# Output and next state in one step, two copies dropped, whole-tile units in the second tile, and the last output in three parts

## The chip, the cores and the metric

The kernel runs on one core of one Trainium2 chip. The time is device microseconds, the median of three runs of the whole program. In the profile PE is the matrix engine and PEld its weight loads, DVE, ACT and POOL are the three elementwise engines, and SP issues the DMAs.

## The reference

Three stages run one after the other on 4 sequences of 768 positions. The first is a chunked linear attention with decay (8 heads of 32 columns, state of 16 rows a head); its output, seen as 3072 tokens of 256 values, goes through two feed-forward layers.

```python
cum = np.cumsum(la, axis=-1)                          # per chunk, la = log(clip(a))
L = np.exp(cum[:, :, :, None] - cum[:, :, None, :]) * causal
M = np.einsum('bhin,bhjn->bhij', Cc, Bc) * L
y = np.einsum('bhij,bhjd->bhid', M, xc) + np.einsum('bhin,bhnd->bhid', Cc, state) * exp(cum)
state = decay_full * state + sum_j(Bc x xc * decay_from_j)
...
h = np.maximum(np.maximum(x @ w1, x @ w2), x @ w3)    # d_ff 768, float64 weights
x = h @ w_out
h = x @ w_in                                          # d_ff 2048
g = np.maximum(h, 0.0) + alpha * np.minimum(h, 0.0)
out = g @ w_out
```

## The kernel before

The tokens are cut into six tiles of 512. The attention is cut into 24 **rounds** of 128 positions of one sequence, so four rounds make a tile's input `xt`. A round has these pieces of PE work, with the lines by which the profile shows them: transposes T of the inputs (L331), the products CB of the two state vectors (L422 in rounds 0 to 11, L412 from round 12 on, where the round is one chunk of 128 instead of two of 64), the output Y (L496 and L504, later L480 and L483), and the state update U (L455, later L441). Around them ACT takes the exponentials (L400, L395), DVE multiplies (L427, L414) and writes `xt` (L514), POOL masks and scales, and SP loads the inputs `b`, `c`, `xm` and the decay rows `e`. From round 12 on, SP also sends two operands through DRAM and back into `bs` and `cs`, and `att_r` then copies both on DVE onto themselves (L372).

The feed-forward work is cut into **units**, one block of 128 hidden features for a number of tokens. Every fp32 product is made of three products of rounded halves, so a first-layer unit has 18 products `up` (3 weights, 2 halves of the input, 3 terms) and 6 products `down` (`acc`), all on L572; a second-layer unit has 6 and 6. `PHASES` gives the order: first layer of tiles 0 and 1, then second layer of tile 0, first layer of tile 2, and so on. Tiles 0 and 1 are cut into two units of 256 tokens for each feature block (`SPLIT`, 12 units a tile), the others into units of 512.

The weights come as float64. They are fetched in 28 pieces of 512 KB into the three `st` buffers, and `convert` turns each piece into two float32 halves in four steps on DVE and ACT (L156 to L171). `next_weights(pace)` hands out one step after each product group.

The order is written in Python: after each unit `quota` says how many attention steps of the list `todo` are due so that the rounds are done when a tile needs them, and `until` forces those that are late. A step is one lambda of `rounds`. A scheduler then moves instructions ahead where its own model of the engines says that they are ready, so each engine's order isn't word for word that of the Python loop; on the chip each engine takes its instructions in that fixed order.

Of the kernel before, what the change touches and what calls it, by code (L numbers as in the profile page):

```python
# [9 lines left out]
F32 = mybir.dt.float32  # L10
# [4 lines left out]
AF = mybir.ActivationFunctionType  # L15
# [4 lines left out]
P = 128  # L20
BT, H, S, D, N = 4, 8, 768, 32, 16
DM = H * D
# [3 lines left out]
NR = BT * NB  # L26
FF1, FF2 = 768, 2048
NF1, NF2 = FF1 // P, FF2 // P
NT = BT * S // 512

SPLIT, WHOLE = ((0, 256), (256, 256)), ((0, 512),)
PHASES = [(1, 0, SPLIT, 1), (1, 1, SPLIT, 1)]
for _t in range(NT):
    PHASES += [(2, _t, WHOLE, 1)] + [(1, _t + 2, WHOLE, 1)] * (_t + 2 < NT)

LEAD = 6144
START = 4
LAG = 2
NX = 3

C_ID, C_PAR, C_PM, C_N = 0, 128, 130, 132
C_TU, C_TS, C_TW, C_SEL, C_T = 0, 128, 256, 512, 1024
NPA = 2
SUMS = 0
WIDE = 20
ORDER = [(0, 0), (1, 0), (0, 1), (1, 1), (2, 0), (2, 1)]
BW = 2
WARM = 8
# [23 lines left out]
def fused(ctx: ExitStack, tc: tile.TileContext, x, a, B, C, w1, w2, w3, w_out, v_in, v_out, alpha, cst, out):  # L72
    nc = tc.nc
# [41 lines left out]
    def st_tile():  # L115
        return stage.tile([P, 1024], U32, tag="st", name="st", bufs=3)
# [60 lines left out]
    steps = convert()  # L177
    ready = [0]

    def need(i):  # L180
        while ready[0] <= i:
            next(steps)

    def next_weights(n):
        for _ in range(n):
            next(steps, None)


    cum_d = dr.tile([NQ, BT * H, Q], F32, name="cum_d", bufs=1)
# [86 lines left out]

    def wide_sums(half):

        if half == 0:
            nc.sync.dma_start(s_c[:, C_TW:C_SEL], cst[:, C_N + C_TW:C_N + C_SEL])  # L280
        ks = slice(3 * half, 3 * half + 3)
        cols = slice(3 * P * half, 3 * P * (half + 1))
        pc = ptile(ps_at, "at", (BT * H, 3 * P))
        for k in range(3):
            nc.tensor.matmul(pc[:, k * P:(k + 1) * P], s_la[:, 3 * half + k, :], s_c[:, C_TW:C_TW + P], start=True, stop=True)
        nc.scalar.activation(s_a[:, cols], pc, AF.Copy)
        nc.sync.dma_start(cum_w[:, cols], s_a[:, cols])
# [64 lines left out]
    def att_l(r):  # L352
# [6 lines left out]
        for c in range(4):  # L359
# [4 lines left out]
                cs[o].bitcast(F32).rearrange("q v e t -> q v (e t)"),  # L364
                sc[:, h:h + 2, :].rearrange("(v q) e t -> q v (e t)", v=4),
            )

    def att_r(r):
        if r < NDIR:
            return  # L370
        for t in (blk[r]["bs"], blk[r]["cs"]):
            nc.vector.tensor_copy(t, t.bitcast(F32))  # L372

    def first_e(r):

# [141 lines left out]
    def rounds(r0):  # L517

        for r in range(r0, NR):
            def first(r=r):  # L520
                if r + 1 < NR:
                    att_l(r + 1)
                if r + 2 < NR:
                    att_a(r + 2)
            yield first, 0
            yield lambda r=r: att_y(r), r + 1
            if r + 1 < NR:
                yield lambda r=r: att_e(r + 1), 0
                yield lambda r=r: (att_r(r + 1), att_u(r + 1)), 0
                yield lambda r=r: att_b(r + 1), 0  # L530
            if r + 2 < NR:
                yield lambda r=r: (att_t(r + 2), load(r + 3)), 0
# [8 lines left out]
    def until(blocks):  # L541
        while y_done[0] < blocks:
            attend()
# [5 lines left out]
    def units_of(ph):  # L549

        layer, t, tokens = ph[:3]
        if len(tokens) == 1:
            cut = [(f, 0, 512) for f in range(NF1 if layer == 1 else NF2)]
        else:
            cut = [(f, *tokens[h]) for q, h in ORDER for f in (2 * q, 2 * q + 1)]
        return [(f, o, n, (24 if layer == 1 else 12) * n, (4 * t + (o + n) // P) * (layer == 1)) for f, o, n in cut]

    def quota(i):

        most, ahead, own = 0.0, 0, plan[i][3]  # L560
        for _, _, _, cols, blocks in plan[i:]:
            most = max(most, left(blocks) * own / max(own, ahead - LEAD))
            ahead += cols
        return most


    def parts(acc, wh, wl, rhs, first, last):
# [16 lines left out]
        return gh[:, :n], gl[:, :n]  # L584

    def up1(ph, f, o, n):
        t, pace = ph[1], ph[3]
        fs = slice(f * P, (f + 1) * P)
        g = un.tile([P, 512], F32, tag="g", name="g")[:, :n]
        for j in range(3):  # L590
            need(4 * (f // 2) + j)
            p = up_mm([w[:, j, :, fs] for w in w123], xt[t], o, n)
            if j == 0:
                nc.scalar.activation(g, p, AF.Copy)  # L594
            else:
                nc.vector.tensor_tensor(g, p, g, ALU.max)  # L596
            next_weights(pace)
        return halves(g, n)

    def up2(ph, f, o, n):  # L600
        t, pace = ph[1], ph[3]
# [6 lines left out]
        next_weights(pace)  # L608
        return halves(g, n, nc.vector if t == NT - 1 and f == NF2 - 1 else nc.gpsimd)

    acc = {}
# [24 lines left out]
    def end2(ph, lo=0, n=512):  # L636
        t = ph[1]
        z = [v_tile().bitcast(F32) for _ in range(2)]
        nc.scalar.activation(z[0][:, :n], acc[2, t][0][:, lo:lo + n], AF.Copy)
        nc.vector.tensor_copy(z[1][:, :n], acc[2, t][1][:, lo:lo + n])  # L640
        base = 512 * t + lo

        def finish(i):
            p = ps_up.tile([P, 2, DM], F32, tag="up", name="up")
            for j in range(2):
# [3 lines left out]
            o = st_tile().bitcast(F32)[:, :512].rearrange("p (j d) -> p j d", j=2)  # L649
            if i % 2:  # L650
                nc.vector.tensor_copy(o, p)
            else:
                nc.scalar.activation(o, p, AF.Copy)
            row = base + 2 * i * P
            nc.sync.dma_start(out[row:row + 2 * P, :].rearrange("(j p) d -> p j d", p=P), o)
        tail.extend(lambda i=i: finish(i) for i in range(n // 256))

    junk = ps_up.tile([P, 512], F32, tag="up", name="up")

# [60 lines left out]
    if True:  # L720
        nc.sync.dma_start(alph, alpha.rearrange("(k p) -> p k", p=P))
        todo += [(go, 0) for go in (
            lambda: att_a(2), lambda: (att_t(2), load(3)), lambda: att_e(2),
            lambda: att_u(2), lambda: att_b(2), lambda: att_a(3), lambda: (att_t(3), load(4)),
        )]
        todo.insert(SUMS, (lambda: list(sums(1)), 0))
        todo += rounds(2)
        for i, go in enumerate((lambda: wide_sums(0), lambda: wide_sums(1), wide_back)):
            todo.insert(WIDE + 3 * i, (go, 0))
        plan = [u for ph in PHASES for u in units_of(ph)]  # L730

        owed, at = 0.0, 0
        for ph in PHASES:
            layer, t, _, pace = ph
            up, end = (up1, end1) if layer == 1 else (up2, end2)
            pend = []
            for f, o, n, _, blocks in units_of(ph):
                until(blocks)
                pend.append((f, o, n, up(ph, f, o, n)))
# [6 lines left out]
                next_weights(pace)  # L746
                owed += quota(at)
                at += 1
                while owed > 0.999 and todo:
                    owed -= 1  # L750
                    attend()
            for i, u in enumerate(pend):
                def go(ph=ph, u=u, finish=end if i == LAG - 1 else None):
                    down(ph, *u)
                    if finish:
                        finish(ph)
                carry.append(go)
        for go in tail:
# [35 lines left out]
```

## Time and profile before

| | us |
|---|---|
| median of 3 runs (lowest to highest) | 569.25 (569.04 to 570.7) |
| time of the profiled execution | 569.79 |
| its span, first to last instruction | 568.0 |
| PE busy | 553.3 (97%) |
| DVE, ACT, POOL busy | 338.4 (60%), 234.7 (41%), 226.9 (40%) |

The granted clock of PE is 0.999 over the span. The ends of matmuls are modelled and overlap, so a PE that shows busy can still be waiting; the time from one start to the next is what a product costs. In the timeline below a row's first number is its start, so the cost of a block is read as the start of the row behind it less the start of the last product before it, less one product.

### The profile page before, as it was taken

The numbers are of one execution on the slowest core, as the hardware profiler recorded it, in microseconds if no ns is written. First come the engines' busy times: TensorE is split into PE (matmuls) and PEld (weight loads), VectorE is DVE, ScalarE is ACT, GpSimd is POOL, SyncE is SP. The second block draws the span as 40 slices with busy tenths as digits, with TensorE's granted clock in tenths as the row PEclk, the third lists the DMA queues.
The fourth block names the chain that finished last, engine by engine and source line by source line (L and its number), as shares of the span: only waits on it lengthen the run. The fifth ranks groups of instructions, "written<-read, shape, count | busy, mean of one in ns | idle before, by whom it ended". The sixth has DMA issues, their size and how long they took to land.

```text
span 568.0 us, 10190 instructions
## 1 busy us (share of the span) xinstructions
PE 553.3 (97%) x3754; PEld 446.3 (79%) x3754; DVE 338.4 (60%) x633; ACT 234.7 (41%) x598; POOL 226.9 (40%) x238
## 2 busy tenths in 40 slices
PE   8989999999999999999999999999999999999996
PEld 4769798897777887777787887787777888888885
DVE  5887899847564446765546664545664325555553
ACT  5667679744233334242543333534322222223222
POOL 2144343445444235453324553423444123444441
PEclk9999999999999999999999999999999999999999
DMA  7888887612213426325354325244110010000001
GB/s 145 222 164 161 233 214 211 144 30 38 31 43 87 111 66 140 86 59 136 73 134 111 89 50 139 65 113 112 38 55 1 1 37 2 0 2 18 20 0 37
DMA packets 118928, 48.53 MB, mean 85 GB/s; under 512 B 80736, under 2 KB 108832, under 8 KB 118880
## 3 DMA queue, kind: packets, MB, share of 16 engines
q1 hardware_dynamic: 118880, 47.90, 34.8%
q8 instruction: 29, 0.48, 0.4%
q14 instruction: 19, 0.16, 0.1%
HBM read 39.82 MB, written 8.06 MB: 84 GB/s over the span
## 4 chain that ended last, share of the span: by engine, by line
PE 85%; DMA 8%; DVE 3%; ACT 2%; issue 1%; POOL 1%; SPq 0%; DVEq 0%; ACTq 0%; POOLq 0%
PE up L572 45%; PE acc L572 30%; DMA st<-in_moe_w_out_dram 4%; DMA b<-in_B_dram 2%; DMA st<-in_moe_w_in_dram 1%; PE at L412 1%; PE at L483 1%; PE up L648 1%; PE at L331 1%; PE at L504 1%; PE at L422 1%; DVE v L165 1%; DMA e<-cum_w 1%; PE at L496 1%; PE at L480 1%
## 5 line engine op out<-in xcount | busy, mean ns | idle before, releaser
L124 POOL TENSOR_TENSOR gl<-g,gh 128x512 fp32r<-128x512 f32 (+1 forms) x143 | 173.0, 1210 | 262.8 <-ACT gh L123 236.2
L123 ACT ACTIVATE gh<-g 128x512 fp32r<-128x512 f32 (+1 forms) x144 | 85.6, 594 | 239.1 <-DVE g L607 157.9
L572 PE MATMUL up<-xt,w 128*128 128x256 f32 (+1 forms) x864 | 166.0, 342 | 3.3 <-ACT g L594 2.7
L572 PEld LDWEIGHTS up<-xt,w 128*128 128x128 f32 x864 | 134.5, 189 | 25.4 <-ACT g L594 3.5
L572 PE MATMUL up<-yt,vi 128*128 128x512 f32 x576 | 151.1, 396 | 0.0
L572 PEld LDWEIGHTS up<-yt,vi 128*128 128x128 f32 x576 | 105.4, 188 | 24.0 <-issue 2.0
L606 DVE TENSOR_SCALAR g<-up,alph 128x512 f32<-128x512 f32 x96 | 72.0, 750 | 87.4 <-PE up L572 81.5
L572 PE MATMUL acc<-gh,vo 128*128 128x512 f32 (+1 forms) x388 | 119.6, 389 | 0.6 <-DVE yt L634 0.5
L596 DVE TENSOR_TENSOR g<-up,g 128x256 f32<-128x256 f32 (+1 forms) x96 | 53.2, 554 | 69.2 <-PE up L572 67.9
L572 PEld LDWEIGHTS acc<-gh,vo 128*128 128x128 f32 x388 | 72.2, 188 | 16.3 <-DVE yt L634 1.4
L572 PE MATMUL acc<-gl,vo 128*128 128x512 f32 (+1 forms) x194 | 75.2, 388 | 0.0
L607 DVE SCALAR_TENSOR_TENSOR g<-up,g 128x512 f32<-128x512 f32 x96 | 66.3, 691 | 3.0
L572 PE MATMUL acc<-gh,wo 128*128 128x256 f32 (+1 forms) x192 | 49.2, 342 | 0.4 <-ACT gh L123 0.2
L572 PEld LDWEIGHTS acc<-gl,vo 128*128 128x128 f32 x194 | 36.4, 188 | 7.8 <-DVE gl L124 0.2
L572 PEld LDWEIGHTS acc<-gh,wo 128*128 128x128 f32 x192 | 32.5, 190 | 4.4 <-ACT gh L123 0.4
L594 ACT ACTIVATE g<-up 128x256 f32<-128x256 f32 (+1 forms) x48 | 23.4, 487 | 30.3 <-PE up L572 27.3
L572 PE MATMUL acc<-gl,wo 128*128 128x256 f32 (+1 forms) x96 | 32.5, 338 | 0.0
L395 ACT ACTIVATE e<-e,ncum 128x128 f32<-128x128 f32 x96 | 30.4, 391 | 3.5 <-DMA e<-cum_w 3.5
L514 DVE TENSOR_TENSOR xt<-at,xt 128x128 fp32r<-128x128 f32 x48 | 11.9, 286 | 20.2 <-ACT xt L513 20.2
L165 DVE SCALAR_TENSOR_TENSOR v<-st,v 128x512 uint32<-128x512 uint32 x28 | 21.6, 773 | 1.0 <-ACT st L156 0.5
L396 POOL TENSOR_SCALAR_AFFINE_SELECT e<-e 128x512 f32<-128x512 f32 x24 | 15.7, 653 | 16.2 <-ACT e L395 12.9
L400 ACT ACTIVATE e<-e,ncum 128x64 f32<-128x64 f32 x80 | 21.4, 342 | 1.1 <-DMA e<-cum_d 1.0
(120 smaller groups left out, 440.3 us busy)
## 6 DMA issues: line engine op xcount, KB each, us to landing
e<-cum_w SPq DMA_DIRECT2D x24, 256.0 KB, 4.1
st<-sc SPq DMA_DIRECT2D x48, 128.0 KB, 2.6
st<-in_moe_w_out_dram SPq DMA_DIRECT2D x11, 512.0 KB, 4.5
st<-in_moe_w_dram SPq DMA_DIRECT2D x9, 512.0 KB, 5.0
sc<-ts SPq DMA_DIRECT2D x12, 384.0 KB, 2.3
st<-in_moe_w_in_dram SPq DMA_DIRECT2D x8, 512.0 KB, 4.4
v<-sc SPq DMA_DIRECT2D x48, 64.0 KB, 2.4
out_dram<-st SPq DMA_DIRECT2D x12, 256.0 KB, 2.2
```

The source lines that it names most:

```text
L123: nc.scalar.activation(dst_h, src, AF.Copy)
L124: engine.tensor_tensor(dst_l, src, dst_h, ALU.subtract)
L165: nc.vector.scalar_tensor_tensor(v, hi, 3, v, ALU.logical_shift_left, ALU.bitwise_or)
L395: nc.scalar.activation(e[:, q, :], e[:, q, :], AF.Exp, bias=ncum[:, k, b, 4 * g + q:4 * g + q + 1])
L396: nc.gpsimd.affine_select(out=e, in_=e, pattern=[[0, 4], [1, P]], compare_op=ALU.is_ge, fill=0.0, base=0, channel_multiplier=-1)
L400: nc.scalar.activation(e[:, h, :], e[:, h, :], AF.Exp, bias=ncum[:, k, b, h:h + 1])
L514: nc.vector.tensor_tensor(xt[t][1][:, g, o], yp[g], xt[t][0][:, g, o], ALU.subtract)
L572: nc.tensor.matmul(acc, w, r, start=(first and i == 0), stop=(last and i == len(todo_) - 1), skip_group_check=True)
L594: nc.scalar.activation(g, p, AF.Copy)
L596: nc.vector.tensor_tensor(g, p, g, ALU.max)
L606: nc.vector.tensor_scalar(g, p, 0.0, alph[:, f:f + 1], ALU.min, ALU.mult)
L607: nc.vector.scalar_tensor_tensor(g, p, 0.0, g, ALU.max, ALU.add)
```

## The change

- `PHASES`: tile 1 is cut into whole units of 512 tokens; tile 0 stays split. Only tile 0 hands out conversion steps at a fixed pace; everywhere else `quota_w` sets the pace by what the coming units need.
- `rounds`: Y of round r and U of round r + 1 are one step; the step that held `att_r` and `att_u` is gone, and so are `att_r` and its two copies.
- The load of the constants for `wide_sums` is issued seven steps into `todo` instead of right ahead of its use, and the three wide sums are put two places earlier (`WIDE`).
- `LAST`: the last feature block's `down` and the output behind it run in parts of 256, 128 and 128 tokens instead of 256 and 256; a part of 128 is copied out half by ACT and half by DVE.

```diff
 SPLIT, WHOLE = ((0, 256), (256, 256)), ((0, 512),)
-PHASES = [(1, 0, SPLIT, 1), (1, 1, SPLIT, 1)]
+LAST = (0, 256), (256, 128), (384, 128)
+PHASES = [(1, 0, SPLIT, 1), (1, 1, WHOLE, 0)]
 for _t in range(NT):
-    PHASES += [(2, _t, WHOLE, 1)] + [(1, _t + 2, WHOLE, 1)] * (_t + 2 < NT)
+    PHASES += [(2, _t, WHOLE, 0)] + [(1, _t + 2, WHOLE, 0)] * (_t + 2 < NT)
+LEADW = 12288
-WIDE = 20
+WIDE = 18
...
+    def slot():
+        owing[0] += owing[1]
+        while owing[0] > 0.999:
+            owing[0] -= 1
+            next_weights(1)
...
-        if half == 0:
-            nc.sync.dma_start(s_c[:, C_TW:C_SEL], cst[:, C_N + C_TW:C_N + C_SEL])
...
-    def att_r(r):
-        if r < NDIR:
-            return
-        for t in (blk[r]["bs"], blk[r]["cs"]):
-            nc.vector.tensor_copy(t, t.bitcast(F32))
...
-            yield lambda r=r: att_y(r), r + 1
+            yield lambda r=r: (att_y(r), r + 1 < NR and att_u(r + 1)), r + 1
             if r + 1 < NR:
                 yield lambda r=r: att_e(r + 1), 0
-                yield lambda r=r: (att_r(r + 1), att_u(r + 1)), 0
                 yield lambda r=r: att_b(r + 1), 0
...
+    def quota_w(i):
+        most, ahead, own = 0.0, 0, plan[i][3]
+        for _, _, _, cols, _, pieces in plan[i:]:
+            most = max(most, (4 * pieces - done[0]) * own / max(own, ahead - LEADW))
+            ahead += cols
+        return most / 4
...
-            next_weights(pace)
+            slot()
...
+            if m == 1:
+                nc.scalar.activation(o[:, :, :P], p[:, :, :P], AF.Copy)
+                nc.vector.tensor_copy(o[:, :, P:], p[:, :, P:])
-            if i % 2:
+            elif i % 2:
...
+        todo[7] = (lambda go=todo[7][0]: (go(), nc.sync.dma_start(s_c[:, C_TW:C_SEL], ...)), 0)
...
-        for o, n in SPLIT:
+        for o, n in LAST:
```

What this does to the engines' orders is shown at three places. On PE, behind the output of round 14 (`xm_107`; L483 is its Y), the second layer of tile 0 goes on at once before the change, and U of round 15 (L441) stands 18 rows further down:

```order
L480 MATMUL at<-cpt,u 64x128 x4
L483 MATMUL at<-e,xm_107 32x128 x8
L572 MATMUL up<-yt_2174,vi_113 128x512 x2
L572 MATMUL up<-yt_2174,vi_114 128x512 x2
L572 MATMUL up<-yt_2175,vi_113 128x512 x2
```

```order
L572 MATMUL acc<-gl,vo_115 128x512
L441 MATMUL at<-xm_105,bp 32x64 x4
L572 MATMUL up<-yt_2174,vi_113 128x512 x2
L572 MATMUL up<-yt_2174,vi_114 128x512 x2
L572 MATMUL up<-yt_2175,vi_113 128x512 x2
```

With the change the same two pieces (now L490 and L448) stand behind each other:

```order
L487 MATMUL at<-cpt,u 64x128 x4
L490 MATMUL at<-e,xm_107 32x128 x8
L448 MATMUL at<-xm_105,bp 32x64 x4
L587 MATMUL up<-yt_1977,vi_113 128x512 x2
L587 MATMUL up<-yt_1977,vi_114 128x512 x2
```

U has moved up to Y. In the whole order U stands directly behind Y in 2 rounds before and in 17 with the change: 5 more of the early kind (L455) and 10 of the late kind (L441), of which none did.

Also on PE, the output of round 6 (here `xm_105`, L504) stands between units of tile 1 before the change; `xt_952` and `xt_953` are the two halves of that tile's input:

```order
L572 MATMUL up<-xt_953,w_0_109 128x256 x2
L572 MATMUL acc<-gh,wo_111 128x256
L572 MATMUL acc<-gh,wo_112 128x256
L572 MATMUL acc<-gl,wo_111 128x256
L572 MATMUL acc<-gh,wo_111 128x256
L572 MATMUL acc<-gh,wo_112 128x256
L572 MATMUL acc<-gl,wo_111 128x256
L496 MATMUL at<-cpt,u 64x64 x4
L504 MATMUL at<-e,xm_105 32x64 x16
L455 MATMUL at<-xm_106,bp 32x128 x4
L572 MATMUL up<-xt_952,w_0_109 128x256 x2
```

With the change it stands among those of tile 0 (`xt_305`, `xt_306`):

```order
L587 MATMUL up<-xt_306,w_0_109 128x256 x2
L587 MATMUL acc<-gh,wo_111 128x256
L587 MATMUL acc<-gh,wo_112 128x256
L587 MATMUL acc<-gl,wo_111 128x256
L587 MATMUL acc<-gh,wo_111 128x256
L587 MATMUL acc<-gh,wo_112 128x256
L587 MATMUL acc<-gl,wo_111 128x256
L503 MATMUL at<-cpt,u 64x64 x4
L511 MATMUL at<-e,xm_105 32x64 x16
L462 MATMUL at<-xm_106,bp 32x128 x4
L587 MATMUL up<-xt_305,w_0_109 128x256
```

Rounds 6 and 7 have moved into tile 0, since a whole unit of tile 1 needs all four rounds at its start: the outputs of rounds 4 to 7 now stand within 162 products of tile 0 behind that of round 3.

On ACT, the end of the program before (L639 takes `acc` out, L653 the transposed output):

```order
L123 ACTIVATE gh<-g 128x512 x14
L639 ACTIVATE v<-acc 128x256 x2
L653 ACTIVATE st<-up 128x512 x2
L790 UNCONDITIONAL_BRANCH
```

and with the change:

```order
L126 ACTIVATE gh<-g 128x512 x14
L655 ACTIVATE v<-acc 128x256
L672 ACTIVATE st<-up 128x512
L655 ACTIVATE v<-acc 128x128
L667 ACTIVATE st<-up 128x128
L655 ACTIVATE v<-acc 128x128
L667 ACTIVATE st<-up 128x128
L813 UNCONDITIONAL_BRANCH
```

The first part's output copy has moved ahead of the second part's `acc` copy, and there are six instructions in a row instead of four.

## Rows read from the trace of the kernel before

**Rows 1.** The page, busy time of each engine (share of the span) and instructions.
```profile
PE 553.3 (97%) x3754; PEld 446.3 (79%) x3754; DVE 338.4 (60%) x633; ACT 234.7 (41%) x598; POOL 226.9 (40%) x238
```

**Rows 2.** Windows of tile 0, tile 1, the rest: engines' busy, clock, DMA share, GB/s.
```profile
20.50:80.40 59.90, 56.38 (x649) 48.51 (x649) 49.45 (x114) 43.72 (x134) 24.56 (x37) 1.00 0.83 186
80.40:126.70 46.30, 43.93 (x498) 39.94 (x498) 35.59 (x80) 32.98 (x98) 21.79 (x29) 1.00 0.56 143
126.70:470.00 343.30, 342.59 (x1999) 271.41 (x1998) 190.16 (x336) 121.36 (x301) 135.55 (x130) 1.00 0.30 75
```

**Rows 3.** Chain that ended last: start, us, what; DMA in tile 1, then 18 products each.
```profile
87.34 4.03 DMA st<-in_moe_w_out_dram
96.87 4.46 DMA st<-in_moe_w_out_dram
...
118.26 2.16 PE up L572 x18
...
175.82 4.08 PE up L572 x18
```

**Rows 4.** Timeline of PE around blocks of rounds: start, us, operation, rows*columns, shape, count.
```profile
81.83 0.28 PE L572 MATMUL acc<-gl,wo 128*128 128x256 f32 x1
82.03 0.34 PE L496 MATMUL at<-cpt,u 32*64 32x64 f32 x8
82.31 0.65 PE L504 MATMUL at<-e,xm 128*32 128x64 f32 x32
82.78 0.40 PE L455 MATMUL at<-xm,bp 128*32 128x128 f32 x8
83.11 1.58 PE L572 MATMUL up<-xt,w 128*128 128x256 f32 x11
...
98.61 0.28 PE L572 MATMUL acc<-gl,wo 128*128 128x256 f32 x1
98.81 0.43 PE L455 MATMUL at<-xm,bp 128*32 128x128 f32 x8
99.17 1.10 PE L572 MATMUL up<-xt,w 128*128 128x256 f32 x7
...
113.93 0.28 PE L572 MATMUL acc<-gl,wo 128*128 128x256 f32 x1
...
115.13 1.10 PE L572 MATMUL up<-xt,w 128*128 128x256 f32 x7
...
222.09 0.39 PE L572 MATMUL acc<-gl,vo 128*128 128x512 f32 x1
222.41 0.32 PE L441 MATMUL at<-xm,bp 128*32 128x64 f32 x8
222.66 1.66 PE L572 MATMUL up<-yt,vi 128*128 128x512 f32 x6
```

**Rows 5.** Waits of PE in tile 0, then in tile 1: total us, times, longest.
```profile
PE at L285 <- DMA yt<-in_shape_constants_dram: 0.9, 1, 0.9
...
PE up L572 <- ACT g L594: 2.2, 2, 1.4
```

**Rows 6.** Groups of DVE by form: busy us, mean ns of one, idle before.
```profile
L467 DVE SCALAR_TENSOR_TENSOR u<-u,dec_f 128x64 f32<-128x64 f32 x22 | 10.0, 452 | 0.4
L372 DVE CAST st<-st 128x1024 fp32r<-128x1024 f32 x12 | 9.4, 783 | 0.0
L427 DVE TENSOR_TENSOR e<-at,e 128x256 f32<-128x256 f32 x24 | 9.2, 416 | 4.3 <-POOL e L403 2.7 <-PE at L422 1.4
L372 DVE CAST v<-v 128x512 fp32r<-128x512 f32 x12 | 5.8, 486 | 0.0
```

**Rows 7.** Timeline of SP's queue: the loads of `b` for rounds 4 and 5.
```profile
33.88 0.42 SPq L205 DMA_DIRECT2D b<-in_B_dram  x1
...
41.37 0.52 SPq L205 DMA_DIRECT2D b<-in_B_dram  x1
```

**Rows 8.** Timeline of the last 4 us: last output copy, last DMA issue.
```profile
564.31 0.60 ACT L653 ACTIVATE st<-up 128x512 f32<-128x512 f32 x1 [0.89 <-PE up L648]
564.93 0.37 SPq L655 DMA_DIRECT2D out_dram<-st  x1
```

More of the change, by code (lines that the diff above doesn't have):

```diff
@@ L178, in fused @@
     ready = [0]
+    done = [0]
     def need(i):
         while ready[0] <= i:
-            next(steps)
+            next_weights(1)
     def next_weights(n):
         for _ in range(n):
+            done[0] += 1
             next(steps, None)
+    owing = [0.0, 0.0]
+    def slot():
+        owing[0] += owing[1]
+        while owing[0] > 0.999:
+            owing[0] -= 1
+            next_weights(1)
     cum_d = dr.tile([NQ, BT * H, Q], F32, name="cum_d", bufs=1)
@@ L555, in units_of @@
             cut = [(f, *tokens[h]) for q, h in ORDER for f in (2 * q, 2 * q + 1)]
-        return [(f, o, n, (24 if layer == 1 else 12) * n, (4 * t + (o + n) // P) * (layer == 1)) for f, o, n in cut]
+        return [(f, o, n, (24 if layer == 1 else 12) * n, (4 * t + (o + n) // P) * (layer == 1),
+                 4 * (f // 2) + 4 if layer == 1 else 4 * (NF1 // 2) + 2 * (f // 2) + 2) for f, o, n in cut]
     def quota(i):
         most, ahead, own = 0.0, 0, plan[i][3]
-        for _, _, _, cols, blocks in plan[i:]:
+        for _, _, _, cols, blocks, _ in plan[i:]:
             most = max(most, left(blocks) * own / max(own, ahead - LEAD))
@@ L586, in up1 @@
     def up1(ph, f, o, n):
-        t, pace = ph[1], ph[3]
+        t = ph[1]
         fs = slice(f * P, (f + 1) * P)
@@ L596, in up1 @@
                 nc.vector.tensor_tensor(g, p, g, ALU.max)
-            next_weights(pace)
+            slot()
         return halves(g, n)
     def up2(ph, f, o, n):
-        t, pace = ph[1], ph[3]
+        t = ph[1]
         fs = slice(f * P, (f + 1) * P)
@@ L607, in up2 @@
         nc.vector.scalar_tensor_tensor(g, p, 0.0, g, ALU.max, ALU.add)
-        next_weights(pace)
+        slot()
+        slot()
         return halves(g, n, nc.vector if t == NT - 1 and f == NF2 - 1 else nc.gpsimd)
@@ L641, in end2, with finish @@
         base = 512 * t + lo
-        def finish(i):
-            p = ps_up.tile([P, 2, DM], F32, tag="up", name="up")
-            for j in range(2):
+        def finish(i, m):
+            p = ps_up.tile([P, 2, DM], F32, tag="up", name="up")[:, :m]
+            for j in range(m):
                 o = slice((2 * i + j) * P, (2 * i + j + 1) * P)
@@ L648, in finish @@
                     nc.tensor.transpose(p[:, j, c * P:(c + 1) * P], z[c][:, o], ident)
-            o = st_tile().bitcast(F32)[:, :512].rearrange("p (j d) -> p j d", j=2)
-            if i % 2:
+            o = st_tile().bitcast(F32)[:, :m * DM].rearrange("p (j d) -> p j d", j=m)
+            if m == 1:
+                nc.scalar.activation(o[:, :, :P], p[:, :, :P], AF.Copy)
+                nc.vector.tensor_copy(o[:, :, P:], p[:, :, P:])
+            elif i % 2:
                 nc.vector.tensor_copy(o, p)
@@ L654, in finish @@
             row = base + 2 * i * P
-            nc.sync.dma_start(out[row:row + 2 * P, :].rearrange("(j p) d -> p j d", p=P), o)
-        tail.extend(lambda i=i: finish(i) for i in range(n // 256))
+            nc.sync.dma_start(out[row:row + m * P, :].rearrange("(j p) d -> p j d", p=P), o)
+        tail.extend(lambda i=i: finish(i, min(2, n // P - 2 * i)) for i in range((n + 255) // 256))
     junk = ps_up.tile([P, 512], F32, tag="up", name="up")
@@ L726, in fused @@
         todo.insert(SUMS, (lambda: list(sums(1)), 0))
+        todo[7] = (lambda go=todo[7][0]: (go(), nc.sync.dma_start(s_c[:, C_TW:C_SEL], cst[:, C_N + C_TW:C_N + C_SEL])), 0)
         todo += rounds(2)
@@ L736, in fused @@
             pend = []
-            for f, o, n, _, blocks in units_of(ph):
+            for f, o, n, _, blocks, _ in units_of(ph):
                 until(blocks)
+                owing[1] = pace or quota_w(at)
                 pend.append((f, o, n, up(ph, f, o, n)))
@@ L745, in fused @@
                     down(ph, *pend.pop(0))
-                next_weights(pace)
+                slot()
+                if layer == 2:
+                    slot()
                 owed += quota(at)
```

## The prediction

> **What bounds the kernel now.** I read the page first: PE is busy 97% of the span, no other engine over 60% [rows 1]. So only what PE does, or waits for, can move the time by much. Next the windows by stage: from 126.7 to 470.0 us PE idles 0.7 of 343.3 us, while tile 0 has 3.5 idle us of 59.9 and tile 1 has 2.4 of 46.3 [rows 2]. There DVE is busy 83% and 77%, and in tile 0 the DMA engines 83%. In these two tiles the rounds of the attention, the conversion of the weights and the products compete; after them PE has its work nearly without a gap. Busy PE isn't useful PE, though, so the third view is the timeline from start to start, which shows what a block of small products costs between two large ones. It is the view on which the largest term rests.
>
> **Merging tile 1's units.** 18 products of 256 columns take 2.16 us from start to start, 0.120 each; 18 of 512 take 4.08, 0.227 each [rows 3]. A pair of the former gives way to one of the latter, 0.240 to 0.227, so 13 ns a pair. Tile 1 has 12 units of 24 products, which become 144: 144 x 0.013 = 1.9 us. The last feature block pays six products more by its third part; a 128-column product costs between half of 0.120 and all of it, and two of them replace one of 256, so 0 to 0.7 us, of which I take 0.1, near the half, as cost goes with columns in the pair above. Term: -1.8.
>
> The Trainium skill ("TensorE: Matmul & The Clock Gate", Back-to-back issue gap) gives columns divided by 2.4 GHz plus 2.5 ns for a product at full clock. By that a pair would save only 2.5 ns, 0.4 us in all, and the sum below would be 1.5 us poorer. The rows read 13 ns a pair with a weight load before every product, and the rows are what I use.
>
> **Y and U in one step.** A U alone costs 99.17 - 98.61 - 0.12 = 0.44 us; a Y alone 115.13 - 113.93 - 0.12 = 1.08; a Y with U right behind it 83.11 - 81.83 - 0.12 = 1.16 [rows 4]. The joined block is that of a round with 8 of the small L496 products where the lone Y has 16; these follow each other within nanoseconds, so I leave that out. A joined U then costs about 0.11 instead of 0.44: entering and leaving a block of small products is paid once. The order shows 5 more such places of the early kind: 5 x 0.33 = 1.65. A late U alone costs 222.66 - 222.09 - 0.227 = 0.34 [rows 4], and no row shows one joined. It saves between 0 and 0.34; I take 0.25, the share of its cost that the early one saves, since both are eight small products. The 10 places give 2.5. Together 4.15; I book 3.9, as two of the early U's already stood against another block of small products. Bounds: 1.4 and 5.1. Term: -3.9.
>
> The Trainium skill ("TensorEngine Tiling (Array Packing)", Key Properties) says that changing the tiling mode drains the engine and that changing only the tile doesn't. The rows read 128*32 for both L504 and L455, and for L441 too, against 128*128 for the products [rows 4]; by the rule nearly all of the 0.34 goes, which would add some 0.5 us to the gain. For a late pair no row here shows it.
>
> **The wide sums' constants.** PE waited 0.9 us for this load once [rows 5]; it now goes out rounds earlier. Term: -0.9, at worst 0. What is late next there are the products themselves.
>
> **Tile 1's waits.** Of its 2.4 idle us, 2.2 were two waits for ACT's first copy L594 [rows 2, 5]. The chain runs there from a weight DMA (4.0 and 4.5 us [rows 3]) through ACT's and DVE's conversion steps into that copy: a conversion stood in the queue ahead of its data and the copy behind it. With whole units there is half the number of copies and two rounds fewer, but DVE's order still has all 28 pieces converted before the second layer of tile 0 begins; the new pace by need moves almost nothing out of tile 1, and I give it no gain. I take -2.0; it can be -2.4, or +1 if the conversions, now 11 pieces in a shorter tile, wait more.
>
> **Tile 0 gets denser.** Rounds 6 and 7 move into it. That moves their PE time (about 2.9 us by the blocks above) from tile 1, which is no change of the sum. What it costs is room on the others. On DVE a round has two L427 and two L467 operations (2 x 0.416 + 2 x 0.452 [rows 6]) and four others which I price at 0.3, about 3 us; two rounds add 6, one piece fewer in the order takes off 2. DVE would then be at (49.5 + 4) of (59.9 + 2.9 - 0.9), 86% after 83%. The cover is still there, but it is thinner, and PE, ACT and DVE each take instructions in a fixed order. I take +1.5. Bounds: -1, if the earlier rounds fill waits, and +8 (the last rival). What queues behind a late Y is every product of tile 0 behind it.
>
> **The copies L372.** 12 x (0.783 + 0.486) = 15.2 us of DVE go [rows 6], from a stretch in which DVE is busy 55% and PE waits for next to nothing [rows 2]. The cover is DVE's idle time: 0, at best -0.7, PE's whole idle time there.
>
> **The end.** The last copy of 0.60 us starts at 564.31 and the last DMA is issued at 564.93; the 3.1 us from there to the end of the span at 568.0 remain [rows 8]. With 128-token parts the last copies are shorter, but ACT's order now has the 0.60 us copy of the first part ahead of the second part's first copy, PE has the third part's products behind the second's transposes, and ACT has six links instead of four. I book +0.2, between -0.8 (the last two copies at half of 0.60 each, and a last DMA of half the bytes) and +0.8 (the first part's 0.60 us copy stands whole in the chain, and a short one more).
>
> **Sum.** -1.8 - 3.9 - 0.9 - 2.0 + 1.5 + 0.2 = -6.9 us. The profiled execution took 569.79 with a span of 568.0; less 6.9 that is 562.9. The median of the runs is 0.5 below that execution, so 562.3.
>
> **Rivals.**
> 1. Only the arithmetic is gained. Tile 0's extra waits eat what tile 1 gives: -2.0 + 1.5 becomes +1, and the late joins save 0.15 instead of 0.25. -6.9 + 1.5 + 1.0 = -4.4, so 564.8. For it speaks DVE's and the DMA engines' 83% in tile 0 [rows 2]; against it that PE idled 3.5 us there all the same, a wait of 0.9 of which goes.
> 2. Everything moved out of the way counts: tile 0 costs nothing, the late joins save all of 0.34, and tile 1's waits vanish. -6.9 - 1.5 - 0.9 - 0.4 = -9.7, and with the end at -0.8 about 558.5. For it speaks how little PE waits once DVE has slack [rows 2]; against it that tile 1 keeps its conversions.
> 3. The hand-out of the conversions does nothing, or harms by running later. The order says the first, and it is in the forecast; as harm it is the +1 of tile 1, within rival 1.
> 4. Slower: the rounds' chain sets tile 0. Rounds 4 to 7 now stand within 162 products, 162 x 0.120 = 19.4 us, plus four rounds' blocks of some 2.3 us (Y with U 1.2, the others about as much), 28.6 us in all. A round is also a chain of loads, ACT, POOL, DVE and PE with two buffers for `b`: where two rounds were back to back the loads stood 41.37 - 33.88 = 7.5 us apart [rows 7]. At that pace four rounds take 30.0 us, 1.4 more than PE's 28.6, which is the +1.5 above. The DMA engines, busy at 83%, get two rounds' loads more. From 9.3 us a round on (4 x 9.3 - 28.6 = 8.6 in place of 1.5) the whole gain is gone; at 10 us it is 11.4, so -6.9 - 1.5 + 11.4 = +3.0 and 572.3. Against it: the 7.5 us was measured with the DMA engines as busy as that, and one weight piece fewer is fetched in tile 0.
>
> **How the numbers follow.** The forecast has 0.55 and by itself reaches from 559.5 to 564; rival 1 has 0.25 (564 to 567.5), rival 2 has 0.12 (557 to 559.5), rival 4 has 0.05, and 0.03 is left for no change at all. The range 557.5 to 567 leaves out rival 4, no change and the edges of the others, under 2 in 10. A change under 0.3%, 1.7 us, is about what can't be told from none here. Faster by more than that: all of the forecast and rival 2, and most of rival 1, 0.90; within it 0.05; slower 0.05.
>
> **What would show it.** Right: no U alone on PE behind round 7, and a late joined block at 1.1 to 1.2 us between products; tile 1's `up` in 512 columns at 0.227; no wait at the wide sums; the start of tile 1's first product at 83 to 85 us, and of the second layer of tile 0 some 38 to 40 us behind it; the last DMA issue about 3.1 us before the end. Wrong: Y of rounds 4 to 7 in the list of PE's waits with several us, or `b` loads over 9 us apart in tile 0 (rival 4); waits for L594 or a weight DMA in tile 1 of over 2 us; late joined blocks that cost 1.38, the sum of both.

## The result and the profile after

The changed kernel took 560.25 us in the median of 4 runs (560.09 to 561.31); the kernel before took 569.14 on the same chip (4 runs, 568.96 to 570.7). The ratio is 0.9842 with a 95% interval of 0.982 to 0.9863: faster by 1.6%, 8.9 us. The forecast was 562.3, with a range of 557.5 to 567. The profiled execution has a span of 559.6 us against 568.0, so the profiles show the same difference, 8.4 us.

PE is busy 545.7 us of it, 98%, and no other engine over 58%. The windows by stage, which answer to [rows 2] (start:end, length, then busy us and instructions of PE, PEld, DVE, ACT, POOL, granted clock, DMA share, GB/s):

```profile
20.50:86.60 66.10, 61.90 (x767) 52.59 (x768) 53.98 (x126) 47.70 (x151) 27.26 (x42) 0.97 0.79 173
86.60:126.30 39.70, 38.23 (x300) 30.19 (x299) 34.87 (x63) 28.70 (x73) 17.55 (x19) 1.00 0.66 170
```

Tile 0 is 6.2 us longer and tile 1 is 6.6 us shorter. PE now idles 4.2 us in tile 0 (3.5 before) and 1.5 in tile 1 (2.4 before). A third window with a fixed end, as in [rows 2], can't show a gain. For that another cut is needed, which follows the work. **First tiles** runs from the first product of tile 0 to the first product of a second layer, **middle** from there to the start of the last `gh` copy on ACT, **end** from there on. The same view of both kernels with that cut, before first:

```profile
20.50:125.10 104.60, 98.71 (x1140) 87.12 (x1140) 84.28 (x191) 76.70 (x231) 45.89 (x65) 1.00 0.73 170
125.10:559.50 434.40, 433.69 (x2407) 346.83 (x2404) 239.92 (x406) 143.87 (x338) 177.23 (x163) 1.00 0.24 61
559.50:568.00 8.50, 4.03 (x25) 3.02 (x23) 1.54 (x3) 2.53 (x5) 0.00 (x0) 0.91 0.18 62
```

```profile
20.50:123.50 103.00, 97.33 (x1055) 80.45 (x1055) 86.47 (x183) 76.22 (x224) 43.45 (x59) 0.98 0.74 173
123.50:550.50 427.00, 426.80 (x2348) 347.96 (x2345) 224.40 (x379) 142.67 (x334) 176.17 (x163) 1.00 0.24 61
550.50:559.60 9.10, 4.93 (x31) 3.69 (x29) 2.19 (x6) 2.49 (x7) 0.00 (x0) 1.00 0.17 58
```

First tiles -1.6, middle -7.4, end +0.6, together -8.4. Two more profiles of the changed kernel (the controls below) have 105.1 and 105.3 us in the first tiles and 427.9 and 427.0 in the middle, so one pair of profiles can't show less than about 2.4 us in the former and 1 us in the latter. By the forecast's terms the first tiles should have given 4.7 to 5 us (merge, constants, waits, early joins, less the denser tile 0) and the middle 2.5 (late joins). The sum is near, and the split isn't; the rest of this text is about that.

PE's waits in tile 0, which answer to [rows 5] (engine, line, who was waited for: total us, times, longest):

```profile
PE at L503 <- DVE e L434: 1.0, 1, 1.0
PE at L429 <- DVE xt L521: 0.7, 1, 0.7
PE at L462 <- DVE bs L363: 0.6, 1, 0.6
...
PE at L298 <- DVE u L468: 0.4, 1, 0.4
```

The wait for the constants' DMA at the wide sums is gone (L298 is one of them now). In tile 1 the list has two rows, of which the longer is a wait of 1.1 us for DVE's L611; for ACT's copy (now L609) PE waits 0.3 us. PE's timeline (start, us, operation, rows*columns, shape, count, [idle before]) shows it, and DVE's timeline shows what stood ahead of L611. The last fence is ACT's timeline before the change, ahead of the longest wait for its copy:

```profile
115.17 1.65 PE L587 MATMUL up<-xt,w 128*128 128x512 f32 x6 [0.33 <-ACT g L609]
117.96 3.03 PE L587 MATMUL up<-xt,w 128*128 128x512 f32 x12 [1.14 <-DVE g L611]
```

```profile
114.56 0.41 DVE L166 TENSOR_SCALAR v<-st 128x512 uint32<-128x512 uint32 x1
114.89 0.68 DVE L174 TENSOR_TENSOR vo<-v,vo 128x512 fp32r<-128x512 f32 x1
115.49 0.68 DVE L168 SCALAR_TENSOR_TENSOR v<-st,v 128x512 uint32<-128x512 uint32 x1
116.10 0.41 DVE L166 TENSOR_SCALAR v<-st 128x512 uint32<-128x512 uint32 x1
116.61 0.69 DVE L168 SCALAR_TENSOR_TENSOR v<-st,v 128x512 uint32<-128x512 uint32 x1
117.22 0.68 DVE L611 TENSOR_TENSOR g<-up,g 128x512 f32<-128x512 f32 x1
```

```profile
108.10 0.67 ACT L156 ACTIVATE st<-st 128x512 f32<-128x512 f32 x1 [1.56 <-DMA st<-in_moe_w_out_dram]
```

Five conversion steps stand in a row in DVE's fixed order, 2.7 us from 114.56 to 117.22, and the copy that frees PE's buffer comes behind them. Before, a conversion ahead of the copy on ACT waited 1.56 us for its weights; these five wait for no data and are simply many.

The blocks, which answer to [rows 4], an early joined one first and then a late one:

```profile
100.98 0.39 PE L587 MATMUL acc<-gl,wo 128*128 128x512 f32 x1
101.29 0.47 PE L503 MATMUL at<-cpt,u 32*64 32x64 f32 x16
101.70 0.65 PE L511 MATMUL at<-e,xm 128*32 128x64 f32 x32
102.17 0.40 PE L462 MATMUL at<-xm,bp 128*32 128x128 f32 x8
102.50 4.39 PE L587 MATMUL up<-xt,w 128*128 128x512 f32 x18
...
208.74 0.39 PE L587 MATMUL acc<-gl,wo 128*128 128x512 f32 x1
209.06 0.45 PE L487 MATMUL at<-cpt,u 32*64 32x128 f32 x8
209.44 0.65 PE L490 MATMUL at<-e,xm 128*32 128x128 f32 x16
209.90 0.29 PE L448 MATMUL at<-xm,bp 128*32 128x64 f32 x8
210.12 1.65 PE L587 MATMUL up<-yt,vi 128*128 128x512 f32 x6
...
212.98 1.52 PE L587 MATMUL up<-yt,vi 128*128 128x512 f32 x6
```

By the reading of the forecast the early joined block costs 102.50 - 100.98 - 0.227 = 1.29 us and the late one 210.12 - 208.74 - 0.227 = 1.15.

And the end, which answers to [rows 8], on ACT:

```profile
550.49 0.63 ACT L126 ACTIVATE gh<-g 128x512 fp32r<-128x512 f32 x1 [2.09 <-DVE g L622]
552.32 0.38 ACT L655 ACTIVATE v<-acc 128x256 f32<-128x256 f32 x1 [1.20 <-PE acc L587]
553.65 0.60 ACT L672 ACTIVATE st<-up 128x512 f32<-128x512 f32 x1 [0.94 <-PE up L664]
554.14 0.27 ACT L655 ACTIVATE v<-acc 128x128 f32<-128x128 f32 x1
555.14 0.28 ACT L667 ACTIVATE st<-up 128x128 f32<-128x128 f32 x1 [0.73 <-PE up L664]
555.31 0.27 ACT L655 ACTIVATE v<-acc 128x128 f32<-128x128 f32 x1
556.36 0.28 ACT L667 ACTIVATE st<-up 128x128 f32<-128x128 f32 x1 [0.78 <-PE up L664]
```

The last copy is half as long, but a further pair of links (0.17 + 0.27 + 0.78 us) lies ahead of it.

### The profile page after: what moved, and what is told of

Read it like the earlier page. It is cut to its first block, busy times and chain, and to the rows that moved or that the text cites. A ratio compares the mean times of both kernels' runs of the same rounds, so it can differ in the third digit from the quotient of the medians.

```text
span 559.6 us, 9832 instructions
## 1 busy us (share of the span) xinstructions
PE 545.7 (98%) x3615; PEld 441.4 (79%) x3616; DVE 325.7 (58%) x600; ACT 233.0 (42%) x588; POOL 223.4 (40%) x232
## 4 chain that ended last, share of the span: by engine, by line
PE 85%; DVE 6%; ACT 3%; issue 2%; DMA 2%; SPq 1%; POOL 0%; DVEq 0%; POOLq 0%; ACTq 0%
PE up L587 46%; PE acc L587 31%; DVE v L168 2%; PE at L490 1%; PE up L664 1%; PE at L344 1%; PE at L419 1%; DMA st<-in_moe_w_dram 1%; SPq L232 1%; DVE g L611 1%; DMA e<-cum_w 1%; PE at L487 1%; PE up L682 1%; DVE v L166 1%; PE at L503 1%
## 5 line engine op out<-in xcount | busy, mean ns | idle before, releaser
L587 PE MATMUL up<-xt,w 128*128 128x512 f32 (+1 forms) x756 | 164.0, 366 | 2.6 <-DVE g L611 1.1
L587 PEld LDWEIGHTS up<-xt,w 128*128 128x128 f32 x756 | 128.6, 190 | 27.7 <-issue 2.9
L587 PE MATMUL up<-yt,vi 128*128 128x512 f32 x576 | 148.9, 394 | 0.0
L611 DVE TENSOR_TENSOR g<-up,g 128x512 f32<-128x512 f32 (+1 forms) x84 | 51.5, 613 | 71.7 <-PE up L587 71.0
L587 PE MATMUL acc<-gh,wo 128*128 128x512 f32 (+1 forms) x168 | 47.4, 366 | 0.2 <-ACT gh L126 0.2
L587 PEld LDWEIGHTS acc<-gh,wo 128*128 128x128 f32 x168 | 29.6, 189 | 4.9 <-ACT gh L126 0.4
L609 ACT ACTIVATE g<-up 128x512 f32<-128x512 f32 (+1 forms) x42 | 22.5, 535 | 24.0 <-PE up L587 21.0
L587 PE MATMUL acc<-gl,wo 128*128 128x512 f32 (+1 forms) x84 | 30.3, 361 | 0.0
L521 DVE TENSOR_TENSOR xt<-at,xt 128x128 fp32r<-128x128 f32 x48 | 12.9, 287 | 19.2 <-ACT xt L520 19.2
L410 POOL TENSOR_SCALAR_AFFINE_SELECT e<-e 64x512 f32<-64x512 f32 x20 | 15.8, 792 | 13.0 <-ACT e L407 12.3
```

Of the source, the lines that this page charges most:

```text
L410: nc.gpsimd.affine_select(out=m, in_=m, pattern=[[0, H], [1, Q]], compare_op=ALU.is_ge, fill=0.0, base=0, channel_multiplier=-1)
L521: nc.vector.tensor_tensor(xt[t][1][:, g, o], yp[g], xt[t][0][:, g, o], ALU.subtract)
L587: nc.tensor.matmul(acc, w, r, start=(first and i == 0), stop=(last and i == len(todo_) - 1), skip_group_check=True)
```

## The experiments

The twelve runs were timed in three sets of four, each on another chip and beside the kernel before, which took 567.7 to 568.1 us in the median there (565.9 to 572.1). The changed kernel itself served as control in the second and third set; the first set, with the four kernels that undo one part, has none. The changed kernel's three medians (560.25 above, 561.96 and 560.78 here) differ by up to 1.7 us, so differences of about 1 us between sets say little.

**Undoing one part at a time.** First U in a step of its own again, behind `att_e`:

```diff
-            yield lambda r=r: (att_y(r), r + 1 < NR and att_u(r + 1)), r + 1
+            yield lambda r=r: att_y(r), r + 1
             if r + 1 < NR:
                 yield lambda r=r: att_e(r + 1), 0
+                yield lambda r=r: att_u(r + 1), 0
```

> The changed kernel, with U of the next round back in a step of its own behind the exponentials, as before the change; no copies. Theory A (a block of small products pays for entering and leaving, so the join is worth what the blocks show): in the changed kernel's trace a late joined block costs 1.155 us, Y alone 1.043, U alone 0.341 before the change, so 0.23 a place, and the second product behind each block comes 0.11 late, so 0.34 a place; 10 late places and 5 early ones (1.297 joined, 1.078 and 0.445 apart, 0.22 + 0.11) give 5.0 us: about 565.3. The recorded term of 3.9 gives 564.2. Rival B (the gain comes from the new order and the dropped copies, and the blocks' cost is hidden): within 0.5 of 560.3.

561.25 us, ratio 0.9891 (0.9869 to 0.9913). The controls below are at 0.9892 and 0.9862, so the join, the largest term of the forecast, is worth nothing that the times can tell. In the profile it is worth much, with both signs. The windows of the first tiles and of the middle without the join:

```profile
20.10:117.90 97.80, 95.01 (x999) 78.67 (x999) 83.70 (x180) 74.49 (x218) 44.35 (x58) 0.98 0.79 181
117.90:550.70 432.80, 432.71 (x2403) 347.54 (x2401) 225.92 (x382) 144.70 (x338) 176.84 (x163) 1.00 0.24 61
```

With the join the first tiles are 5.2 us longer (103.0; 7.3 and 7.5 in the controls) and the middle is 5.8 shorter (427.0). 56 matmul records more lie in the first tiles (1055 and 999): the 48 of an early Y and the 8 of its U, a block of 1.3 us that the order has moved there from the middle. PE's idle time grows from 2.8 to 5.7 us, and without the join PE has no wait at all in tile 1. So about 4.5 us is what the middle gains by itself, and about 3.9 what the first tiles lose in this pair, three quarters of it as waits.

The edit undoes less on PE than it says. In this trace U still stands right behind its Y at 42, 64 and 72 us, where the scheduler put it; of the early places it separates four (55, 102, 123 and 145 us in the changed kernel's trace), and all ten late ones.

The copies back, ahead of `att_b`:

```diff
-                yield lambda r=r: att_b(r + 1), 0
+                yield lambda r=r: (att_r(r + 1), att_b(r + 1)), 0
```

> The changed kernel, with the two copies of the operands put back, right ahead of the CB products. Theory A (the prediction's: DVE's idle time covers them): 0, 560.3. Rival B (they stand between the DMA's landing and the CB products, and held PE by waits too short to show as idle): late CB blocks cost 0.56 us on average before the change and 0.472 in every one of them after it, some 1.2 us in all: 561.4, with CB blocks (four products of 256) longer than 0.48 us in the timeline again.

561.0 us, 0.9889 (0.9864 to 0.9914); its middle stretch is 427.5 us against 427.0. DVE's busy time there rises from 224 to 236 us, and PE's idle time stays at 0.1 to 0.2. The copies cost 0 to 0.5 us.

Tile 1 in halves again:

```diff
-PHASES = [(1, 0, SPLIT, 1), (1, 1, WHOLE, 0)]
+PHASES = [(1, 0, SPLIT, 1), (1, 1, SPLIT, 0)]
```

> The changed kernel, with tile 1 cut into units of 256 tokens again. That moves rounds 6 and 7 back into tile 1. Theory A (whole units gain their 13 ns a pair and tile 1's waits; tile 0's denser rounds cost less than that): 1.9 + about 2, so 564. Rival B (what tile 1 gains is lost in tile 0, which in the changed kernel's trace took 6 us more, of which only some 2.9 are moved work): between 559 and 561, tile 0 near 60 us again and tile 1 near 45.

563.7 us, 0.9925 (0.9908 to 0.9943): whole units are worth 1.7 to 2.9 us beside the two controls of the other sets, with the join there.

The end in two parts again:

```diff
-LAST = (0, 256), (256, 128), (384, 128)
+LAST = SPLIT
```

> The changed kernel, with the last output in two parts of 256 tokens again. The recorded term says that three parts cost 0.2 us: 560.1. The changed kernel's trace has 9.1 us from the last rounding copy on ACT to the end of the span, 8.5 before the change: then 559.7. Rival (smaller last parts pay): 560.9 or more.

560.47 us, 0.9875 (0.9853 to 0.9896). The end stage is 8.54 us instead of 9.11 in the profile. So the third part costs 0.57 us, which the medians can't separate but which recurs in every profile (8.53 or 8.54 with two parts, 9.11 to 9.13 with three).

**The control**, the changed kernel again:

> The changed kernel itself, as the measure for the others of this group, since chips differ by a few tenths of a per cent: 0.984 of the kernel before, and in the profile 60.5 us of waits and small blocks up to the 77th us of products, 31 from there to the 340th.

561.96 us, 0.9892 (0.9871 to 0.9914), where 0.984 was expected.

**One part alone in the kernel before.** Only the join (`att_r` moves to `att_b`):

```diff
-            yield lambda r=r: att_y(r), r + 1
+            yield lambda r=r: (att_y(r), r + 1 < NR and att_u(r + 1)), r + 1
...
-                yield lambda r=r: (att_r(r + 1), att_u(r + 1)), 0
-                yield lambda r=r: att_b(r + 1), 0
+                yield lambda r=r: (att_r(r + 1), att_b(r + 1)), 0
```

> The kernel before with only the join of Y and the next U; the copies and the split tile 1 stay. The recorded term for the join alone is -3.9. Theory A (late places give 0.34 each, early ones cost about 3 us by the buffers): -1 to -2 in all, with the stretch behind tile 1 some 4 us shorter and tiles 0 and 1 some 2 to 3 longer. Rival B (the join gives its 5 us everywhere): -5.

568.12 us, 0.9998 (0.9979 to 1.0018): nothing, as in the changed kernel. First tiles 106.6 us (104.6 before), middle 427.9 (434.4). But this profile is of its fastest execution, 564.4 us, and the others reach 570.3; where the median loses what the profile shows as a gain is not shown.

Only the whole units of tile 1:

```diff
-PHASES = [(1, 0, SPLIT, 1), (1, 1, SPLIT, 1)]
+PHASES = [(1, 0, SPLIT, 1), (1, 1, WHOLE, 1)]
```

> The kernel before with only tile 1 in whole units, at the fixed pace. Recorded terms: -1.9 for the products, -2.0 for tile 1's waits, +1.5 for the denser tile 0: -2.4. Theory A (only the products' arithmetic remains, the rest goes out evenly): -1.9. Rival B (tile 0's rounds become the bound): +1 or more.

562.94 us, 0.9914 (0.9894 to 0.9934): this one line gives 5.1 us of the whole. First tiles in its profile:

```profile
20.40:117.80 97.40, 94.41 (x997) 78.31 (x998) 84.97 (x181) 75.05 (x218) 45.21 (x58) 1.00 0.78 182
```

7.2 us shorter than before, with 3.0 us of PE's idle time where there were 5.9. The two profiles differ by 7.8 us, the medians by 5.1, so the stage overstates the gain.

**Where the join pays.** U apart up to round 7 and joined from round 8 on, with the end in two parts:

```diff
-            yield lambda r=r: (att_y(r), r + 1 < NR and att_u(r + 1)), r + 1
+            yield lambda r=r: (att_y(r), 8 <= r < NR - 1 and att_u(r + 1)), r + 1
             if r + 1 < NR:
                 yield lambda r=r: att_e(r + 1), 0
+                if r < 8:
+                    yield lambda r=r: att_u(r + 1), 0
```

> The changed kernel, with U of the next round apart from Y up to round 7 and joined from round 8 on, and the last output in two parts. Theory A (a joined U saves its share of a block everywhere, but in tiles 0 and 1 it takes the third of the three small PSUM buffers, and the next CB waits for DVE to clear one): tiles 0 and 1 as in the kernel with all U apart (some 3 us shorter), the later stretch as in the changed kernel (31 us of waits and blocks), the end 0.57 shorter: 560.3 - 3.1 - 0.6 = 556.6. Rival B (tiles 0 and 1 were shorter there only because a round lay later): 559.5, the control less the end.

556.72 us, 0.9806 (0.9785 to 0.9827), the fastest of all. Its windows:

```profile
20.50:120.30 99.80, 94.56 (x997) 77.82 (x998) 85.56 (x181) 74.79 (x219) 44.33 (x58) 1.00 0.77 177
120.30:548.20 427.90, 427.90 (x2403) 348.93 (x2402) 224.73 (x380) 144.17 (x338) 176.48 (x163) 1.00 0.24 62
```

The middle keeps the gain, and the first tiles get back 3.2 of the 5.2 us; they hold the same matmuls as with U apart everywhere (997 and 999 records), and the 2.0 us by which they are longer than there are within what profiles of one kernel differ by.

The opposite kernel, joined up to Y of round 7 and apart from round 8 on:

```diff
-            yield lambda r=r: (att_y(r), r + 1 < NR and att_u(r + 1)), r + 1
+            yield lambda r=r: (att_y(r), r < 8 and att_u(r + 1)), r + 1
             if r + 1 < NR:
                 yield lambda r=r: att_e(r + 1), 0
+                if r >= 8:
+                    yield lambda r=r: att_u(r + 1), 0
```

> The changed kernel, but Y and U are one step only for Y of rounds 2 to 7; from Y of round 8 on, U is a step of its own again. With the join in no round 561.3 us was measured, with it from round 8 on (and the last output in two parts) 556.7, with it everywhere 562.0. Theory A: the early joins cost about 4.5 us in tiles 0 and 1, and the late ones give about 5. Then this kernel has only the cost: 565 to 567, with some 105 us from the first product to the first of the second layer, and a middle stretch of 433. Theory B: the early joins cost nothing by themselves, and 556.7 was a lucky order of one program: 560.5 to 562.

565.2 us, 0.9953 (0.9933 to 0.9973), as theory A has it. Four kernels now stand in a square, all with three parts at the end (0.57 added to the one with two):

| | late U apart | late U joined |
|---|---|---|
| early U apart | 561.25 | 557.3 |
| early U joined | 565.2 | 561.96 and 560.78 |

Joining the late ones gives 3.2 to 4.4 us in either row, and joining the early ones costs 3.5 to 4.7 in either column. The kernels of the square come from three sets, but one comparison of each kind lies within a set: 565.2 to 560.78 for the late joins, 557.3 to 561.96 for the early ones. The stages of this profile agree only in part: first tiles 102.5 (97.8 with none joined), middle 431.4.

In these two traces one can see what "early joined" is. On PE U stands right behind Y at 43, 53, 65 and 72 us, one place more (53 us) than with U apart, so the place behind Y isn't the difference. What differs is the order of the rest: Y of those rounds stays behind almost the same number of products of the feed-forward layers, while a later U comes behind 255 of them instead of 300, and the pieces behind it, Y and U of the next rounds among them, mostly 12 or 24 products earlier. Up to the transposes behind the 252nd product both take 57 us, though U apart has a stretch at half clock in it, told below. From there to the first product of a second layer, U apart first:

```profile
77.30:117.90 40.60, 40.60 (x323) 32.44 (x321) 37.32 (x69) 32.13 (x85) 20.26 (x22) 1.00 0.72 184
```

```profile
77.50:122.90 45.40, 42.60 (x371) 33.23 (x369) 40.59 (x73) 34.30 (x92) 19.85 (x22) 1.00 0.65 170
```

Of the 4.8 us, 2.8 are waits of PE, which has none with U apart, and 1.1 a Y more (48 records). So in this pair the early cost shows where the moved order meets the end of tile 0 and tile 1. One Python step fewer a round also moves what `quota` hands out, and no run tells that from the place of U itself (an empty step in place of U's would).

Joined from round 6 on:

```diff
-            yield lambda r=r: (att_y(r), 8 <= r < NR - 1 and att_u(r + 1)), r + 1
+            yield lambda r=r: (att_y(r), 6 <= r < NR - 1 and att_u(r + 1)), r + 1
...
-                if r < 8:
+                if r < 6:
```

> The changed kernel with U in a step of its own up to Y of round 5, joined from round 6 on, and the last output in two parts. With the join from round 8 on 556.7 was measured. Theory A: what the early joins cost lies in rounds 2 to 5, at 36 to 50 us, where tile 0 starts: 556.5 to 557. Theory B: each early join costs its share, 4.6 us by 6 rounds, 0.77 each: two more joins give 558.3.

558.32 us (555.25 to 559.26), 0.9815 (0.9783 to 0.9847). The median speaks for theory B, the profiled span of 557.0 for theory A, and the interval holds both. It didn't tell them apart.

The second control, in one set with the kernels joined up to round 7 and from round 6 on and with the next one:

> The changed kernel itself, as the control of the others on this chip: 561 to 562.5 if the chip is like that of the last runs, 560.3 if it is like that of the first measurement.

560.78 us, 0.9862 (0.983 to 0.9893).

**Why do early joins cost?** Behind a joined block Y's two buffers and U's one are all three small PSUM buffers, and in tile 0 the next CB waits 0.7 us for DVE's L521 once. To test that, the early U wrote into a buffer of the large products:

```diff
-        up = ptile(ps_at, "at", (P, 2, 2, D))
+        up = ps_up.tile([P, 512], F32, tag="up", name="up")[:, :4 * D].rearrange("p (c h d) -> p c h d", c=2, h=2)
```

> The changed kernel, but the early U writes its sum into one of the three PSUM buffers of the large products instead of one of the three small ones; the scheduler moves some pieces of tile 0 with it. Theory A: behind a joined block, Y's two buffers and U's one leave no small buffer for the next piece (CB or T), which therefore waits for ACT and DVE; with U elsewhere the next piece can begin, and 3 to 4.5 us come back: 557.5 to 559 where the changed kernel has 562. Theory B: the buffers aren't it, but the place of U ahead of the other pieces in the queues of POOL and DVE: 561 to 563, and tiles 0 and 1 together as long as before this edit.

567.86 us, 1.0001 (0.998 to 1.0022): 7 us slower, which neither theory had. Three things came with the edit. The rounds' pieces moved: the outputs that stood behind 90 products of tile 0 now stand behind 72. The products now wait for the buffer that U holds, and the granted clock is about half of full in three stretches of the first tiles (0.52 at 25 to 32 us, 0.53 at 45.6 to 49.2 and at 113.8 to 117.4). The longest wait of PE, and the window of the first tiles:

```profile
PE up L587 <- DVE u L468: 2.9, 2, 2.5
```

```profile
19.70:131.00 111.30, 101.35 (x1054) 83.14 (x1054) 86.23 (x182) 76.20 (x224) 44.51 (x59) 0.94 0.68 161
```

So the run says that this was a bad place for U, and nothing about the small buffers. The 0.7 us wait for L521 also stands in the kernel with U apart. What the traces show of the early cost is the waits: no wait of PE in tile 1 with U apart, 1.5 us with the join, 1.1 of it behind a run of conversion steps on DVE. For the rest the cause stays open.

## Why the prediction was right, and which step of it was wrong

- **What bounds the kernel**: right. PE sets the time in each of the twelve runs, and in the middle of the kernels whose windows are shown it idles 0.7 us at most (1.1 in one control).
- **Merging tile 1**: right in price, since 18 products of 512 columns took 4.1 us here as in [rows 3]. The whole units as such were worth more in the kernel before, 5.1 us where the merge, tile 1's waits and the denser tile 0 were booked at -2.4 together (-1.9, -2.0, +1.5). Rounds 6 and 7 in tile 0 cost next to nothing when U stays apart: PE's idle time in the first tiles fell by 2.9 us, more than the 2.0 booked, and no +1.5 came back. So rival 4 was far off, and so was the term that is its mild form. What the rest of the 5.1 us is, is not shown.
- **Y and U in one step**: this is the step that failed. The forecast priced it by its arithmetic on PE alone, "5 x 0.33 = 1.65" for the early ones and 2.5 for the late. The late ones were under-priced. A late Y alone costs 206.90 - 205.63 - 0.227 = 1.04 and a U alone 215.53 - 214.97 - 0.227 = 0.33 without the join (rows below), the joined block 1.15, which saves 0.22; but the six products behind any such block take 1.65 instead of 1.52 us, 0.13 more, and that too is now paid once. 10 x 0.35 = 3.5; 3.2 to 4.4 us were measured, and 4 to 4.9 in the middle stages of the profiles. The early ones were given the wrong sign: joining them costs 3.5 to 4.7 us. The forecast counted places at which U stands behind Y and assumed that nothing else moves; the join also moves the later pieces ahead, in two tiles where DVE is 82% and 88% busy, and PE waits more. That DVE's load is why it costs there and pays later is likely, but no run shows it. The forecast had named such a price for the rounds that move into tile 0 and left it out for U. A smaller slip lies in "so I leave that out": a joined block with 16 of the small L496 products (L503 now) costs 1.29 and not 1.16. The Trainium skill ("TensorEngine Tiling (Array Packing)", Key Properties) has it that a change of the tile without a change of mode doesn't drain the engine; the joined U costs 1.15 - 1.04 = 0.11 of its 0.33 us, so most of it goes, as the rule says. The rows are from the kernel with U apart, Y first and then U:

```profile
205.63 0.39 PE L588 MATMUL acc<-gl,wo 128*128 128x512 f32 x1
...
206.90 1.66 PE L588 MATMUL up<-yt,vi 128*128 128x512 f32 x6
...
214.97 0.39 PE L588 MATMUL acc<-gl,vo 128*128 128x512 f32 x1
215.28 0.32 PE L448 MATMUL at<-xm,bp 128*32 128x64 f32 x8
215.53 1.66 PE L588 MATMUL up<-yt,vi 128*128 128x512 f32 x6
```

- **The wide sums' constants**: half right. The wait of 0.9 us for the load is gone, but what was late next were not "the products themselves" but U's evacuation on DVE, 0.4 us, which leaves 0.5.
- **Tile 1's waits**: half right in the changed kernel. Of 2.4 idle us 1.5 remain, and the place of ACT's copy is taken by DVE's, behind five conversions. The wait behind "a conversion stood in the queue ahead of its data" is gone, and one behind a busy queue has come. Without the join the whole term came true.
- **Tile 0**: +1.5 was booked, too little with the join. The tile is 6.2 us longer; the forecast's own 2.9 of moved work leaves 3.3, where it had 1.5 less the constants' 0.9. PE's idle time grew by 0.7 there, though the wait of 0.9 is gone, and a stretch at half clock, told below, adds 1.0 to 1.7. Without the join tile 1's first product comes 61.6 us behind tile 0's, against 58.1 before: 3.5 more, 0.6 above the moved work, and that trace has such a stretch too.
- **The copies**: right, 0 to 0.5 us by which the middle is longer with them.
- **The end**: +0.57 instead of +0.2, within its bounds. The further pair of links on ACT outweighs the shorter copies, and also the last DMA of half the bytes, which is issued 2.6 us before the end of the span instead of 3.1.

Why the sum still fits: the joins were booked at -3.9 and gave about 0; the whole units with their side effects were booked at -2.4 and gave -5.1 alone, -1.7 to -2.9 beside the join. Two errors of opposite signs nearly cancel, which is luck. The parts don't add up, either: taken alone they give 0 + 5.1 + 0.5 - 0.57, 5.0 us, with the copies at most 5.5, and the change gave 6.1 and 6.9 us beside the controls and 8.9 in the first measurement; and with tile 1 split again, 4.3 us are left where the join alone gave nothing. The new hand-out of the conversions, booked at 0, and the moved load of the constants were not tested by themselves. So the time was right, and its two largest terms, the joins and tile 1's waits, were not.

## What to carry to other kernels

Moving a step in a fixed order moves the steps behind it too, on every engine, so the saving at the place that is read isn't its whole price: price it separately for each stage, test it there, and apply it only where it pays. Here the join from round 8 on with the end in two parts takes 556.7 us, against 562.0 for the change as made in the same set. When the cost of a block is read from start to start, the products behind the block belong to it as well.

## What the runs showed of the hardware

In nine of the fourteen profiles the granted clock fell once in tile 0 to half of full, 1.2 GHz, for 3.4 us, at 42 to 48 us; in the kernel before it didn't. In the changed kernel (windows as above):

```profile
39.00:42.40 3.40, 1.85 (x18) 1.41 (x17) 2.24 (x6) 2.32 (x8) 2.27 (x5) 1.00 0.45 84
42.40:44.20 1.80, 1.80 (x54) 1.24 (x50) 1.63 (x4) 0.64 (x3) 0.73 (x1) 1.00 0.76 149
44.20:47.60 3.40, 3.40 (x26) 3.05 (x26) 2.03 (x6) 2.58 (x10) 0.06 (x1) 0.51 0.95 205
```

PE was busy 1.85 of 3.40 us, then wholly busy, and only then the clock was 0.51. In that stretch the timeline has 17 products of 256 columns:

```profile
45.53 3.22 PE L587 MATMUL up<-xt,w 128*128 128x256 f32 x17
48.59 0.28 PE L344 MATMUL at<-ct,b 128*128 128x128 f32 x1
```

They took 3.06 us from start to start where 0.120 each would be 2.04. These alone lost 1.0 us, and the whole stretch up to 1.7, half of its 3.4. Such a stretch of waits isn't always followed by a fall: the kernel before had PE busy 1.75 of 3.00 us at 40 to 43 us and kept 1.00.

```profile
40.00:43.00 3.00, 1.75 (x30) 1.15 (x33) 2.15 (x6) 1.28 (x5) 1.96 (x4) 1.00 0.67 204
```

The kernel joined up to round 7 also kept 1.00 there and was slow all the same, and the kernel with U apart had the fall and was faster, so the clock doesn't explain the early joins' cost. In the experiment with U in the products' buffer three such stretches lay in the first tiles.
